# A gated-attention and MLP kernel: the third and fourth unit's matmuls reordered with nine more warm-ups, and two strided access patterns turned round

## The chip, the cores and the metric

The kernel runs on one core of a Trainium2 chip. Its time is the device time of one execution in microseconds (us). Three executions before the change took 475.53, 478.7 and 479.36 us; the median, 478.7 us, is what the changed kernel is compared with.

## The reference

Two stages, in float32. The first is a gated linear recurrence for 4 batches x 8 heads, 768 steps, head size 48. The second is a two-layer network on the 3072 resulting rows.

```
f = 1 / (1 + exp(-f_logit))
for t in range(S):
    state = f[:, :, t, :, None] * state + einsum('bhd,bhe->bhde', k[:, :, t], v[:, :, t])
    y[:, :, t] = einsum('bhd,bhde->bhe', q[:, :, t], state)
x = y.transpose(0, 2, 1, 3).reshape(3072, 384)
h = x @ w_in                      # 384 -> 2048
g = h * clip(h + 3, 0, 6) / 6
out = g @ w_out                   # 2048 -> 384
```

## The kernel before, in words

**Units and groups.** The sequence is cut into 6 chunks of 128 steps. A chunk of one batch is a unit (24 units, numbered from 0), and the four units of a chunk make a group of 512 token columns. Units 0 to 3, the first unit of each batch, have an empty state. For each unit VectorE (DVE in the profile) runs a backward scan over the gates (`back`, L350), takes reciprocals (`rend`), runs a forward scan (`fwd`, L374), and keys and queries are scaled (`kmul` L363, `qmul` L379, on VectorE or on GpSimd, POOL in the profile). TensorE (PE) then computes the scores (`att`, L418), which VectorE masks (`mask`, L425); turns the keys (`tk`, L437), which ScalarE (ACT) copies out (`ktok`); multiplies turned keys with values (`kv`, L456), from which the state is carried on (`carry0`, `carry1`: L469 and L476 on ScalarE for units 0 to 3); and multiplies queries with the state (`qs`, L488) and masked scores with values (`av`, L505). ScalarE copies the result as the high half of a float32r pair (`xh`, L524); for the first units TensorE subtracts that high half in PSUM (`ym`, L528), and ScalarE copies the rest (`xl`, L535). `hole` moves 16 rows of heads by DMA to where the network's first product wants them.

**The network.** For each group and each of 16 blocks of 128 hidden units there are nine matmuls `mm1` (L573), `relu` on ScalarE (L583), `g` on VectorE (L587), a split of the result into a high and a low half (`gh` L596, `gl` L600), and nine matmuls `mm2` (L617) into three PSUM banks `o`. All large products are three float32r products of high and low halves. The weights' halves are made on the core from the raw input (`ld`, `cy`, `z`, `mid`, `lim`, `dif`, `top`, `high`, `low`), during the first 110 us. The first three blocks of the first group are done in halves of 256 columns: half `a` for units 0 and 1, half `b` for units 2 and 3 (`mm1a`, `relua`, `ga`, `mm2a` and the same with `b`). Here `relu` (L644) and `g` (L648) work on tiles `th` of 256 columns, and `mm2` (L653) is a plain float32 product, without a split. The products' 512 columns are held with two batches woven together: `turned` reads the first product's input so, and `halves_of` turns the order of the second product's input as it is read. When a group is complete its three banks are copied out (`outs` on ScalarE L687, `outv` on VectorE L685) and stored (`od`); the last group's third bank goes in two halves (`outh`).

**What sets the order.** Each token of the string ORDER (L51) issues one step, in that order, and every engine runs its own instructions strictly in that order (L813). The number behind a second dot is the PSUM bank: 0 and 1 are the two halves of `pair0`, 2 and 3 of `pair1`, 4 is `single`. `warm.n` (L789) issues n bf16 matmuls of zeros of 128x512 into the bank `idle`, whose result nobody reads. Steps that use one PSUM bank from different engines wait for each other (`settle`, L749).

Of the kernel before, what the change touches and what calls it, by code (L numbers as in the profile page):

```python
# [56 lines left out]
warm.1 ym.1 mask.2 kmul.3 rend.3 lowi.0 lim.1 fwd.3 dif.1 qmul.3 warm.1 kv.2.0 tk.3.4 hole.0~carry1.1 loadv.3 load.4  # L57
loadq.4 xl.1 z.2 carry0.2 carry1.2 ktok.3 qs.2.2 av.2 kv.3.0 lim.2 end.3 gate.4 carry0.3 xh.2 carry1.3 hole.1 mid.2
top.1 dif.2 top.2 mm1a.0.4 ym.2 high.1 xl.2 att.3.0 mask.3 warm.1 qs.3.2 warm.1 av.3 lowi.1 mm1a.1.1 ld.3 wd.0~ktok.3
load.5 ld.4~carry0.3 hole.2~wd.0 wd.1 loadq.5 relua.0 high.2 cy.3 xh.3 ym.3 ga.0 relua.1 xl.3 back.4 gate.5 z.3 cy.4  # L60
mid.3 rend.4 kmul.4 lowi.2 hole.3 ld.5 wd.2~hole.3 ga.1 lim.3 dif.3 back.5 mm2a.0 mm1a.2.1 mm2a.1 end.4 lim.4 end.5
z.4 mm1b.0.2 mm1b.1.0 mm1b.2.3 relub.0 relua.2 relub.1 top.3 fwd.4 qmul.4 cy.5 high.3 kmul.5 gb.0 ga.2 gb.1 tk.4.4
ktok.4 z.5 mm2b.0 tk.5.0 mm2a.2 ld.6~relub.0 mid.4 dif.4 top.4 mid.5 low.3 rend.5 high.4 relub.2 ktok.5 lim.5 low.4
fwd.5 dif.5 mm1.3.2 mm2b.1 att.4.0 mm1.4.4 cy.6 lim.6 mid.6 top.5 dif.6 decay.5 gb.2 mm2b.2 loadv.4~cy.5 ld.7
loadv.5~ld.6 loadq.6~loadv.4 z.6 relu.3 top.6 high.5 cy.7 z.7 relu.4 g.3 low.5 decay.4 qmul.5 mask.4 kv.4.2 kv.5.0 g.4
mm1.5.4 carry0.4 carry0.5 carry1.4 carry1.5 gh.3 high.6 load.6~lim.6 ld.8~ld.7 gate.6 ld.9 cy.8 gh.4 relu.5 qs.4.0 z.8
ld.10 loadq.7~z.8 gl.3 back.6 mid.7 low.6 lim.7 att.5.2 av.4 kmul.6 g.5 mask.5 dif.7 gl.4 mm2.3 mm2.4 end.6 lim.8 z.9
gh.5 mid.8 top.7 rend.6 dif.8 top.8 high.7 low.7 gl.5 fwd.6 tk.6.2 ktok.6 cy.9 high.8 low.8 mid.9 mm1.6.3 mm1.7.2
mm1.8.4 load.7~ld.10 ld.11 loadv.6 qmul.6 xh.4 ym.4 z.10 relu.6 g.6 relu.7 gh.6 xl.4 gate.7 g.7 lim.9 mm2.5 qs.5.0
att.6.2 av.5 kv.6.0 gl.6 dif.9 top.9 back.7 cy.10 lim.10 relu.8 mid.10 high.9 z.11 gh.7 xh.5 cy.11 mm2.6 g.8 mask.6  # L70
kmul.7 dif.10 low.9 top.10 high.10 loadv.7 hole.4 ld.12 end.7 cy.12 gh.8 mm1.9.2 mid.11 lim.11 gl.7 dif.11 decay.6
top.11 gl.8 decay.7 mm2.7 tk.7.3 mm2.8 low.10 carry0.6 xl.5 load.8 lim.12 relu.9 g.9 rend.7 carry1.6 ktok.7 z.12 ld.13
ld.14 cy.13 gh.9 fwd.7 mid.12 dif.12 top.12 gl.9 mm1.10.4 qs.6.2 kv.7.0 carry0.7 av.6 qmul.7 z.13 relu.10 xh.6 xl.6
carry1.7 mm2.9 att.7.2 qs.7.0 mid.13 g.10 high.11 cy.14 gate.8 low.11 gh.10 z.14 lim.14 high.12 hole.6 ld.15 load.9
loadv.8 hole.5 mm1.11.4 lim.13 mask.7 gl.10 av.7 mm2.10 dif.13 top.13 mid.14 low.12 xh.7 high.13 relu.11 g.11 low.13
xl.7 cy.15 gh.11 loadv.9 hole.7 loadq.8 loadq.9 loadq.10 mm1.12.2 mm1.13.3 z.15 gl.11 dif.14 top.14 high.14 mid.15
lim.15 dif.15 top.15 low.14 mm2.11 high.15 relu.12 low.15 mm1.14.0 mm1.15.1 mm1.16.4 back.8 g.12 relu.13 relu.14 g.14
rend.8 kmul.8 g.13 gh.12 gate.9 gl.12 end.8 relu.15 gh.13 mm2.12 tk.8.0 gl.13 back.9 fwd.8 mm2.13 gh.14 relu.16 ktok.8
g.15 qmul.8 kv.8.0 att.8.2 load.10 gh.15 kmul.9 decay.8 gl.14 rend.9 mm2.14 gl.15 mask.8 carry0.8 g.16 carry1.8 lowo.0
lowo.2 mm2.15 mm1.17.4 mm1.18.0 mm1.19.1 gh.16 gate.10 outs.0 outs.2 outv.1 fwd.9 gl.16 mm2.16 od.0 tk.9.3 od.2  # L80
relu.17 od.1 back.10 relu.18 end.9 end.10 qmul.9 g.17 rend.10 fwd.10 gh.17 relu.19 ktok.9 g.19 g.18 lowo.1 mm1.20.4
qs.8.0 att.9.2 av.8 kmul.10 qmul.10 decay.9 decay.10 mask.9 gl.17 kv.9.0 mm2.17 tk.10.2 mm1.21.3 xh.8 gh.18 load.11
loadq.11 load.12 loadv.10 gh.19 gl.18 carry0.9 carry1.9 gl.19 xl.8 mm2.18 ktok.10 gate.11 relu.20 relu.21 back.11 g.21
g.20 qs.9.0 att.10.2 av.9 kv.10.0 mm2.19 mm1.22.4 gate.12 back.12 end.12 end.11 gh.20 rend.11 carry0.10 fwd.11 qmul.11
load.13 loadq.12 kmul.11 mask.10 gl.20 tk.11.2 mm2.20 loadv.11 xh.9 relu.22 rend.12 g.22 gh.21 ktok.11 gh.22 gl.21
gl.22 decay.11 fwd.12 carry1.10 mm1.23.4 relu.23 g.23 kmul.12 gate.13 mm2.21 mm1.24.3 gh.23 relu.24 mm2.22 mm1.25.4
qmul.12 gl.23 relu.25 xl.9 g.24 gh.24 qs.10.0 att.11.2 av.10 kv.11.0 xh.10 mask.11 back.13 carry0.11 xl.10 g.25
rend.13 carry1.11 mm2.23 mm1.26.3 tk.12.2 mm1.27.4 ktok.12 relu.26 gl.24 fwd.13 g.26 qs.11.0 att.12.2 av.11 hole.10
load.14 loadv.12 kv.12.0 loadq.13 loadv.13 qmul.13 mask.12 decay.12 gh.25 xh.11 gate.14 relu.27 xl.11 back.14
carry0.12 rend.14 carry1.12 gl.25 mm2.24 hole.11 hole.9 load.15 gh.26 fwd.14 gl.26 g.27 hole.8 loadv.14 loadq.14  # L90
mm1.28.3 mm1.29.2 relu.28 g.28 mm1.30.1 mm1.31.0 mm1.32.3 mm2.25 mm2.26 gh.27 gl.27 mm2.27 gh.28 gl.28 mm2.28 relu.29
end.13 relu.30 kmul.13 g.29 gh.29 kmul.14 g.30 gh.30 gl.29 decay.13 gl.30 tk.13.4 mm2.29 ktok.13 relu.31 g.31 relu.32
tk.14.4 g.32 qs.12.0 att.13.2 av.12 kv.13.0 qmul.14 end.14 ktok.14 gate.15 xh.12 gh.31 decay.14 carry0.13 xl.12
carry1.13 back.15 mask.13 mm1.33.4 mm2.30 qs.13.0 kv.14.2 av.13 hole.12 rend.15 loadq.15 loadv.15 load.16 loadv.16
loadq.16 gl.31 fwd.15 end.15 decay.15 qmul.15 kmul.15 carry0.14 relu.33 g.33 carry1.14 mm2.31 xh.13 xl.13 mm1.34.2
mm1.35.1 tk.15.3 outs.3 gate.16 gh.32 gl.32 back.16 rend.16 od.3 relu.34 gh.33 relu.35 end.16 outs.5 g.34 ktok.15
mm1.36.4 g.35 outv.4 od.5 kmul.16 att.14.2 kv.15.0 gl.33 od.4 relu.36 g.36 carry0.15 carry1.15 mask.14 fwd.16 qmul.16
mm2.32 mm2.33 tk.16.4 gh.34 gh.35 ktok.16 qs.14.2 att.15.0 av.14 kv.16.2 decay.16 gl.35 carry0.16 carry1.16 mask.15
mm1.37.4 xh.14 gl.34 xl.14 mm2.34 qs.15.0 att.16.2 av.15 relu.37 gh.36 gl.36 load.17 load.18 xh.15 mm2.35 mask.16
xl.15 hole.14 loadq.17 hole.15 loadv.17 loadq.18 loadv.18 mm1.38.0 mm1.39.3 mm1.40.2 mm2.36 mm1.41.1 gate.17 gate.18  # L100
back.17 g.37 rend.17 back.18 fwd.17 relu.38 end.17 relu.39 gh.37 gl.37 rend.18 relu.40 kmul.17 fwd.18 kmul.18 g.39
qmul.18 g.40 qmul.17 load.19 hole.13 load.20 mm2.37 tk.17.3 decay.17 g.38 gh.38 ktok.17 gl.38 mm1.42.0 mm2.38 tk.18.2
relu.41 gh.39 gl.39 gh.40 ktok.18 gl.40 g.41 relu.42 g.42 mm1.43.4 relu.43 g.43 mm1.44.2 mm1.45.1 mm1.46.3 mm1.47.0
mm1.48.4 mm2.39 mm2.40 gh.41 gl.41 mm2.41 gh.42 gl.42 mm2.42 relu.44 gh.43 gl.43 g.44 relu.45 relu.46 gh.44 g.45 g.46
gl.44 mm2.43 mm2.44 relu.47 g.47 qs.16.0 att.17.2 av.16 kv.17.0 gh.45 gl.45 mm2.45 gh.46 relu.48 g.48 mm1.49.4 xh.16
end.18 gh.47 gl.46 mm2.46 relu.49 gl.47 g.49 mm1.50.4 relu.50 mm2.47 carry0.17 xl.16 carry1.17 g.50 gh.48 gh.49 outs.6
outs.8 gl.48 outv.7 mask.17 mm1.51.4 od.6 od.8 qs.17.0 att.18.2 av.17 od.7 kv.18.0 relu.51 gl.49 mm2.48 mm2.49 gate.20
xh.17 gh.50 g.51 decay.18 carry0.18 gl.50 carry1.18 mm2.50 gh.51 loadv.19 loadq.19 xl.17 gate.19 gl.51 back.19 rend.19
end.19 mask.18 fwd.19 kmul.19 back.20 mm1.52.4 relu.52 rend.20 g.52 fwd.20 qmul.19 loadv.20 hole.17 loadq.20 mm1.53.0
mm2.51 relu.53 end.20 qmul.20 g.53 kmul.20 decay.19 mm1.54.1 tk.19.2 ktok.19 relu.54 g.54 load.21 load.22 gh.52 gl.52  # L110
gh.53 gate.21 mm1.55.3 relu.55 gl.53 g.55 tk.20.0 ktok.20 mm1.56.4 qs.18.0 att.19.2 av.18 kv.19.0 xh.18 relu.56
mask.19 carry0.19 carry1.19 xl.18 g.56 back.21 decay.20 mm2.52 mm2.53 qs.19.0 att.20.2 av.19 gh.54 gh.55 rend.21 gl.55
gl.54 mask.20 kv.20.0 mm2.54 mm1.57.3 gate.22 end.21 relu.57 fwd.21 hole.16 loadq.21 qmul.21 loadq.22 decay.21 kmul.21
gh.56 gl.56 g.57 carry0.20 mm1.58.4 mm1.59.2 mm2.55 load.23 relu.58 gate.23 tk.21.3 hole.18 loadv.21 loadv.22 ktok.21
# [821 lines left out]
```

## Time and profile before

| | |
|---|---|
| Executions (us) | 475.53, 478.7, 479.36; median 478.7 |
| Profiled execution's own time | 481.13 us |
| Its span | 479.4 us |
| Mean granted TensorE clock | 0.981 |
| Busy: PE, DVE, ACT, POOL | 460.9, 295.9, 225.4, 53.1 us |
| Share of the chain of waits that ended last | PE 80%, DVE 8%, DMA 4%, ACT 4%, issue 2% |
| DMA traffic | 44.91 MB, mean 94 GB/s; the first 12 us at 293 GB/s |

A profile line names the source line, the engine, the operation, the tile written and the tiles read (buffer numbers are left out). A timeline row gives the start in us, the length of a run of like instructions, their count, and in brackets the idle time before them with what ended it; "issue" there is a wait for nothing that the profile shows. A float32 product is two records. A page row of 40 digits cuts the span in 40 slices of 12 us; PEclk is the granted TensorE clock in tenths of full speed. PEld is TensorE's weight load, which runs beside its matmuls.

### The profile page before, as it was taken

The numbers are of one execution on the slowest core, as the hardware profiler recorded it, in microseconds if no ns is written. First come the engines' busy times: TensorE is split into PE (matmuls) and PEld (weight loads), VectorE is DVE, ScalarE is ACT, GpSimd is POOL, SyncE is SP. The second block draws the span as 40 slices with busy tenths as digits, with TensorE's granted clock in tenths as the row PEclk, the third lists the DMA queues.
The fourth block names the chain that finished last, engine by engine and source line by source line (L and its number), as shares of the span: only waits on it lengthen the run. The fifth ranks groups of instructions, "written<-read, shape, count | busy, mean of one in ns | idle before, by whom it ended". The sixth has DMA issues, their size and how long they took to land.

```text
span 479.4 us, 11485 instructions
## 1 busy us (share of the span) xinstructions
PE 460.9 (96%) x4958; PEld 391.5 (82%) x4958; DVE 295.9 (62%) x462; ACT 225.4 (47%) x372; POOL 53.1 (11%) x57
## 2 busy tenths in 40 slices
PE   8879999899999999999999999999999999899994
...
PEclk9959999999999999999999999999999999999998
...
GB/s 293 277 224 214 287 201 183 101 225 58 105 86 84 30 191 0 158 88 146 69 0 2 1 198 77 107 33 2 63 68 10 25 2 0 67 0 1 0 1 72
DMA packets 18969, 44.91 MB, mean 94 GB/s; under 512 B 2528, under 2 KB 8544, under 8 KB 18912
## 3 DMA queue, kind: packets, MB, share of 16 engines
...
q8 instruction: 41, 0.67, 0.6%
q14 instruction: 16, 0.13, 0.1%
q10 hardware_dynamic: 144, 0.13, 0.1%
...
## 4 chain that ended last, share of the span: by engine, by line
PE 80%; DVE 8%; DMA 4%; ACT 4%; issue 2%; SPq 0%; POOL 0%; DVEq 0%; ACTq 0%
PE o L617 32%; PE pair L573 22%; PE single L573 10%; DMA raw<-w 3%; PE pair L488 2%; PE pair L505 2%; PE o L653 2%; PE pair L418 2%; PE pair L456 2%; PE pair L635 1%; PE pair L668 1%; PE single L668 1%; DMA v<-unit 1%; DVE w L285 1%; DVE tg L587 1%
## 5 line engine op out<-in xcount | busy, mean ns | idle before, releaser
L617 PE MATMUL o<-gg,weight 128*128 128x512 f32 x693 | 161.4, 383 | 2.5 <-DVE gg L600 2.4
L617 PEld LDWEIGHTS o<-gg,weight 128*128 128x128 f32 x693 | 128.8, 189 | 22.2 <-DVE gg L600 4.1
L573 PE MATMUL pair<-xts,weight 128*128 128x512 f32 x576 | 132.7, 381 | 0.8 <-DVE weight L293 0.8
L573 PEld LDWEIGHTS pair<-xts,weight 128*128 128x128 f32 x576 | 107.5, 189 | 16.3 <-DVE weight L293 1.2
L600 DVE TENSOR_TENSOR gg<-tg,gg 128x512 fp32r<-128x512 f32 x77 | 53.8, 703 | 58.2 <-ACT gg L596 57.9
L596 ACT ACTIVATE gg<-tg 128x512 fp32r<-128x512 f32 x77 | 48.1, 627 | 82.6 <-PE o L617 59.8
L587 DVE SCALAR_TENSOR_TENSOR tg<-tg,pair 128x512 f32<-128x512 f32 x64 | 42.8, 682 | 48.7 <-ACT tg L583 48.7
L583 ACT ACTIVATE tg<-pair,half 128x512 f32<-128x512 f32 x64 | 43.1, 683 | 54.3 <-PE pair L573 46.2
L573 PE MATMUL single<-xts,weight 128*128 128x512 f32 x261 | 62.2, 383 | 0.0
L573 PEld LDWEIGHTS single<-xts,weight 128*128 128x128 f32 x261 | 48.4, 189 | 6.7
L374 DVE TENSOR_TENSOR_SCAN gates<-gates,rend 112x516 f32<-112x516 f32 x24 | 33.2, 1382 | 0.2
L350 DVE TENSOR_TENSOR_SCAN suffix<-gates,unit 112x516 f32<-112x516 f32 x24 | 30.4, 1265 | 2.8 <-ACT gates L344 2.8
L583 ACT ACTIVATE tg<-single,half 128x512 f32<-128x512 f32 x29 | 19.7, 679 | 22.9 <-PE single L573 19.2
L363 POOL TENSOR_TENSOR qkf<-qkf,suffix 112x512 f32<-112x512 f32 x13 | 17.9, 1375 | 94.9 <-DVE suffix L350 34.4
L524 ACT ACTIVATE xts<-pair 112x512 fp32r<-112x512 f32 x24 | 14.3, 594 | 26.1 <-PE pair L456 12.2
L379 POOL TENSOR_TENSOR qkf<-qkf,gates 112x512 f32<-112x512 f32 x13 | 16.6, 1282 | 81.7 <-PE o L617 46.1
L587 DVE SCALAR_TENSOR_TENSOR tg<-tg,single 128x512 f32<-128x512 f32 x29 | 19.7, 679 | 9.3 <-ACT tg L583 9.3
L617 PE MATMUL o<-xts,weight 128*128 128x512 f32 x96 | 23.7, 381 | 1.6 <-ACT xts L596 1.5
L425 DVE TENSOR_TENSOR a<-pair,causal 128x512 f32<-128x512 f32 x24 | 16.4, 681 | 13.6 <-PE pair L505 8.1
L617 PEld LDWEIGHTS o<-xts,weight 128*128 128x128 f32 x96 | 17.9, 189 | 4.7 <-ACT xts L596 1.9
L537 DVE TENSOR_TENSOR xts<-pair,xts 112x512 fp32r<-112x512 f32 x19 | 13.0, 684 | 10.6 <-ACT xts L524 10.6
L456 PE MATMUL pair<-v,ktok 64*48 64x48 f32 (+1 forms) x768 | 15.0, 213 | 4.7 <-issue 2.7
...
## 6 DMA issues: line engine op xcount, KB each, us to landing
...
```

The source lines that it names most:

```text
L350: nc.vector.tensor_tensor_scan(flat(sf)[:, ::-1], gt[:, 1:][:, ::-1], flat(unit)[:, ::-1], 0.0, op0=ALU.mult, op1=ALU.add,)
L363: engine("kmul", i).tensor_tensor(parts_of(t, 1), parts_of(t, 1), split(sf[:, :, 1:C + 1]), op=ALU.mult)
L374: nc.vector.tensor_tensor_scan(past, past, flat(rend), 0.0, op0=ALU.mult, op1=ALU.add)
L379: engine("qmul", i).tensor_tensor(parts_of(t, 0), parts_of(t, 0), split(to), op=ALU.mult)
L425: nc.vector.tensor_tensor(d["a"].rearrange("r p e t -> r e p t"), d["at"], causal.unsqueeze(1).unsqueeze(1).broadcast_to([128, 2, NP, HC]) ...
L456: nc.tensor.matmul(d["kv"][r:r + m, odd, c, n], d["ktok"][rs, 2 * n + part, r:r + m], heads_of(vt[rs], part, n, e)[:, :D], start=(odd, e) ...
L573: nc.tensor.matmul(h, win(f, a, k), turned(g["xt"][:, k, :g["n"] // C, b]), start=i == 0, stop=i == 3 * KT - 1,)
L583: nc.scalar.activation(d["t"], d["h"], AF.Relu, bias=half, scale=1.0 / 6.0)
L587: nc.vector.scalar_tensor_tensor(d["t"], d["t"], 1.0, d["h"], op0=ALU.min, op1=ALU.mult)
L596: nc.scalar.activation(d["gg"][:, 0], d["t"], AF.Copy)
L600: engine("gl", f if g["name"] == "0" else NU).tensor_tensor(d["gg"][:, 1], d["t"], d["gg"][:, 0].bitcast(F32), op=ALU.subtract)
L617: nc.tensor.matmul(g["o"][m], wout(f, a, m), halves_of(g[f]["gg"][:, b]), start=f == 0 and i == 0, stop=f == NF - 1 and i == 2, skip_group ...
```

## The change

Four edits, two in the table of steps and two in access patterns.

1. Nine more warm-ups: `warm.1` ahead of `kv.2` becomes `warm.6`, and a `warm.2` each is put ahead of `qs.2` and behind `av.2`.
2. `att.3` (the fourth unit's scores) moves from behind `mm1a.0` and `ym.2` to ahead of `kv.3`.
3. The half tiles `th` are held in the order of the output: `relu` and `g` read the PSUM tile with a step of 128 elements and write the tile in a row, and `mm2` reads it in a row. Before, all of that was the other way round.
4. The copies of a finished bank read PSUM with a step of 4 elements and write in a row. Before, they read in a row and wrote with a step of 64 elements.

```
-warm.1 ym.1 mask.2 kmul.3 rend.3 lowi.0 lim.1 fwd.3 dif.1 qmul.3 warm.1 kv.2.0 tk.3.4 ...
+warm.1 ym.1 mask.2 kmul.3 rend.3 lowi.0 lim.1 fwd.3 dif.1 qmul.3 warm.6 kv.2.0 tk.3.4 ...
-... ktok.3 qs.2.2 av.2 kv.3.0 lim.2 ... mm1a.0.4 ym.2 high.1 xl.2 att.3.0 mask.3 ...
+... ktok.3 warm.2 qs.2.2 av.2 warm.2 att.3.0 kv.3.0 lim.2 ... mm1a.0.4 ym.2 high.1 xl.2 mask.3 ...

+    def ranked(x, woven=0):
+        return x.rearrange("p (b c) -> p c b" if woven else "p (c b) -> p c b", b=2)
...
-            nc.scalar.activation(d["t"], d["h"], AF.Relu, bias=half, scale=1.0 / 6.0)
+            nc.scalar.activation(ranked(d["t"]), ranked(d["h"], 1), AF.Relu, bias=half, scale=1.0 / 6.0)
...
-            nc.vector.scalar_tensor_tensor(d["t"], d["t"], 1.0, d["h"], op0=ALU.min, op1=ALU.mult)
+            t = ranked(d["t"])
+            nc.vector.scalar_tensor_tensor(t, t, 1.0, ranked(d["h"], 1), op0=ALU.min, op1=ALU.mult)
...
-                    wout(f, 1, m).bitcast(F32), halves_of(g[f, p]["t"]),
+                    wout(f, 1, m).bitcast(F32), g[f, p]["t"],
...
-            os = os.rearrange("p (h q c) -> p h c q", q=4, c=HC)
-            src = src.rearrange("p (h c q) -> p h c q", q=4, c=HC)
+            os = os.rearrange("p (h q c) -> p h q c", q=4, c=HC)
+            src = src.rearrange("p (h c q) -> p h q c", q=4, c=HC)
```

The first place is TensorE, from the turning of unit 3's keys (`single<-ident`, L437) over unit 2's `qs` and `av` (L488, L505, `pair_71`) to unit 3's `kv` (L456, 24 matmuls of which the first stands here), the first half product (L635, L639 after), unit 2's `ym` (L528) and unit 3's scores (L418, `qkf_328`). Before:

```order
L437 MATMUL single<-ident,qkf_328 128x112 x4
L488 MATMUL pair_71<-qkf_209,middle_102 64x64 x8
L505 MATMUL pair_71<-a_400,v_330 64x64 x8
L505 MATMUL pair_71<-a_400,v_330 48x64 x8
L456 MATMUL pair_70<-v_440,ktok_450 64x48
...
L635 MATMUL single<-xts,weight 128x256 x9
L528 MATMUL pair_71<-xts,minus 112x256 x2
L418 MATMUL pair_70<-qkf_328 64x64 x16
L792 LDWEIGHTS blank
L792 MATMUL idle<-blank 128x512
```

The same place of the changed kernel, where each pair of rows on `blank` stands for two such pairs:

```order
L437 MATMUL single<-ident,qkf_328 128x112 x4
L797 LDWEIGHTS blank
L797 MATMUL idle<-blank 128x512
...
L488 MATMUL pair_71<-qkf_209,middle_102 64x64 x8
L505 MATMUL pair_71<-a_400,v_330 64x64 x8
L505 MATMUL pair_71<-a_400,v_330 48x64 x8
...
L418 MATMUL pair_70<-qkf_328 64x64 x16
L456 MATMUL pair_70<-v_445,ktok_455 64x48
...
L639 MATMUL single<-xts,weight 128x256 x9
L528 MATMUL pair_71<-xts,minus 112x256 x2
```

The scores of unit 3 stand ahead of its `kv`, and two pairs of warm-ups stand on either side of unit 2's `qs` and `av`. Five more pairs stand ahead of unit 2's `kv`, a few rows above. The other engines' order is unchanged.

The second place is ScalarE where the fifth group ends: the copies of its first and third bank (`os<-o`, L687, L692 after), ahead of the first `relu` (L583) of the last group. Before:

```order
L596 ACTIVATE gg_15_4521<-tg_15_4487 128x512
L687 ACTIVATE os_4533<-o_0_4098 128x2x64x4
L687 ACTIVATE os_4533<-o_2_4100 128x2x64x4
L583 ACTIVATE tg_0_4542<-pair_71,half 128x512
L596 ACTIVATE xts<-tg_0_4542 128x512
```

The same place of the changed kernel:

```order
L596 ACTIVATE gg_15_4530<-tg_15_4496 128x512
L692 ACTIVATE os_4542<-o_0_4107 128x512
L692 ACTIVATE os_4542<-o_2_4109 128x512
L583 ACTIVATE tg_0_4551<-pair_71,half 128x512
L596 ACTIVATE xts<-tg_0_4551 128x512
```

Nothing moves here; the two copies write 512 elements in a row instead of runs of four with a step.

More of the change, by code (lines that the diff above doesn't have):

```diff
@@ L56 @@
 cy.1 end.1 carry0.1 carry1.1 gate.3 end.2 high.0 ktok.2 qs.1.2 av.1 xh.1 cy.2 mid.1 qmul.2 back.3 warm.1 att.2.0
[L57 to L114, printed above, removed]
-gh.57 relu.59 xh.19 g.58 xl.19 back.22 kmul.22 g.59 hole.19 mm1.60.4 mm1.61.3 mm2.56 mm1.62.2 mm1.63.0 mm1.64.1 gh.58
@@ L136 @@
-gh.95 mm2m0.94 gl.95 mm2m1.93 mm2m1.94 mm2m0.95 mm2m1.95 outs.15 mm2p.93 od.15 outv.16 mm2p.94 mm2p.95 od.16 mm2q.93
-outh.15 mm2q.94 odh.15 mm2q.95 outh.16 odh.16
+warm.1 ym.1 mask.2 kmul.3 rend.3 lowi.0 lim.1 fwd.3 dif.1 qmul.3 warm.6 kv.2.0 tk.3.4 hole.0~carry1.1 loadv.3 load.4
+loadq.4 xl.1 z.2 carry0.2 carry1.2 ktok.3 warm.2 qs.2.2 av.2 warm.2 att.3.0 kv.3.0 lim.2 end.3 gate.4 carry0.3 xh.2
+carry1.3 hole.1 mid.2 top.1 dif.2 top.2 mm1a.0.4 ym.2 high.1 xl.2 mask.3 warm.1 qs.3.2 warm.1 av.3 lowi.1 mm1a.1.1
@@ new lines @@
+ld.3 wd.0~ktok.3 load.5 ld.4~carry0.3 hole.2~wd.0 wd.1 loadq.5 relua.0 high.2 cy.3 xh.3 ym.3 ga.0 relua.1 xl.3 back.4
+gate.5 z.3 cy.4 mid.3 rend.4 kmul.4 lowi.2 hole.3 ld.5 wd.2~hole.3 ga.1 lim.3 dif.3 back.5 mm2a.0 mm1a.2.1 mm2a.1
+end.4 lim.4 end.5 z.4 mm1b.0.2 mm1b.1.0 mm1b.2.3 relub.0 relua.2 relub.1 top.3 fwd.4 qmul.4 cy.5 high.3 kmul.5 gb.0
+ga.2 gb.1 tk.4.4 ktok.4 z.5 mm2b.0 tk.5.0 mm2a.2 ld.6~relub.0 mid.4 dif.4 top.4 mid.5 low.3 rend.5 high.4 relub.2
+ktok.5 lim.5 low.4 fwd.5 dif.5 mm1.3.2 mm2b.1 att.4.0 mm1.4.4 cy.6 lim.6 mid.6 top.5 dif.6 decay.5 gb.2 mm2b.2
@@ new lines @@
+loadv.4~cy.5 ld.7 loadv.5~ld.6 loadq.6~loadv.4 z.6 relu.3 top.6 high.5 cy.7 z.7 relu.4 g.3 low.5 decay.4 qmul.5 mask.4
+kv.4.2 kv.5.0 g.4 mm1.5.4 carry0.4 carry0.5 carry1.4 carry1.5 gh.3 high.6 load.6~lim.6 ld.8~ld.7 gate.6 ld.9 cy.8 gh.4
+relu.5 qs.4.0 z.8 ld.10 loadq.7~z.8 gl.3 back.6 mid.7 low.6 lim.7 att.5.2 av.4 kmul.6 g.5 mask.5 dif.7 gl.4 mm2.3
+mm2.4 end.6 lim.8 z.9 gh.5 mid.8 top.7 rend.6 dif.8 top.8 high.7 low.7 gl.5 fwd.6 tk.6.2 ktok.6 cy.9 high.8 low.8
+mid.9 mm1.6.3 mm1.7.2 mm1.8.4 load.7~ld.10 ld.11 loadv.6 qmul.6 xh.4 ym.4 z.10 relu.6 g.6 relu.7 gh.6 xl.4 gate.7 g.7
@@ new lines @@
+lim.9 mm2.5 qs.5.0 att.6.2 av.5 kv.6.0 gl.6 dif.9 top.9 back.7 cy.10 lim.10 relu.8 mid.10 high.9 z.11 gh.7 xh.5 cy.11
+mm2.6 g.8 mask.6 kmul.7 dif.10 low.9 top.10 high.10 loadv.7 hole.4 ld.12 end.7 cy.12 gh.8 mm1.9.2 mid.11 lim.11 gl.7
+dif.11 decay.6 top.11 gl.8 decay.7 mm2.7 tk.7.3 mm2.8 low.10 carry0.6 xl.5 load.8 lim.12 relu.9 g.9 rend.7 carry1.6
+ktok.7 z.12 ld.13 ld.14 cy.13 gh.9 fwd.7 mid.12 dif.12 top.12 gl.9 mm1.10.4 qs.6.2 kv.7.0 carry0.7 av.6 qmul.7 z.13
+relu.10 xh.6 xl.6 carry1.7 mm2.9 att.7.2 qs.7.0 mid.13 g.10 high.11 cy.14 gate.8 low.11 gh.10 z.14 lim.14 high.12
@@ new lines @@
+hole.6 ld.15 load.9 loadv.8 hole.5 mm1.11.4 lim.13 mask.7 gl.10 av.7 mm2.10 dif.13 top.13 mid.14 low.12 xh.7 high.13
+relu.11 g.11 low.13 xl.7 cy.15 gh.11 loadv.9 hole.7 loadq.8 loadq.9 loadq.10 mm1.12.2 mm1.13.3 z.15 gl.11 dif.14
+top.14 high.14 mid.15 lim.15 dif.15 top.15 low.14 mm2.11 high.15 relu.12 low.15 mm1.14.0 mm1.15.1 mm1.16.4 back.8 g.12
+relu.13 relu.14 g.14 rend.8 kmul.8 g.13 gh.12 gate.9 gl.12 end.8 relu.15 gh.13 mm2.12 tk.8.0 gl.13 back.9 fwd.8 mm2.13
+gh.14 relu.16 ktok.8 g.15 qmul.8 kv.8.0 att.8.2 load.10 gh.15 kmul.9 decay.8 gl.14 rend.9 mm2.14 gl.15 mask.8 carry0.8
```

78 lines of the change are left out of this document (58 added, 20 removed).

## The prediction

> **What bounds the kernel now.** I read the page's rows by slices first, then busy times by stage, then the timeline of TensorE (PE) where the stages show something odd.
>
> ```profile
> PE   8879999899999999999999999999999999899994
> PEclk9959999999999999999999999999999999999998
> ```
>
> PE is busy nearly everywhere, and its clock is low in one place, the third slice of 12 us. The stages around it, with these columns: length; busy us (and instructions) of PE, PEld, DVE, ACT, POOL; clock; DMA share; GB/s:
>
> ```profile
> 24.56:38.21 13.65, 11.00 (x182) 9.35 (x183) 6.99 (x13) 6.48 (x13) 1.00 (x1) 0.50 0.66 229
> 38.21:58.00 19.79, 19.79 (x138) 15.75 (x141) 18.04 (x29) 19.15 (x29) 5.34 (x4) 1.00 0.73 241
> 84.00:118.00 34.00, 30.87 (x335) 24.94 (x337) 30.94 (x50) 24.15 (x36) 5.47 (x5) 1.00 0.38 132
> 118.00:404.00 286.00, 285.55 (x3174) 248.03 (x3167) 168.16 (x262) 110.46 (x195) 26.93 (x25) 1.00 0.20 65
> ```
>
> From 118 us on PE is the bound (285.55 of 286 us busy at full clock), and nothing in that stage changes but the length of copies on engines that are half idle. From 38.21 to 58 PE, ScalarE (19.15 of 19.79 us) and VectorE (18.04) are all nearly full, so that stage can only start earlier, not shrink much. The first wait that the change can reach is the stretch from 24.56 to 38.21: half clock, PE idle for 2.65 us, ScalarE and VectorE half empty. What PE does there and just before:
>
> ```profile
> 16.30 0.91 PE L456 MATMUL pair<-v,ktok 64*64 64x48 f32 x48 [0.26 <-DMA v<-unit]
> 20.86 0.39 PE L792 MATMUL idle<-blank 128*128 128x512 bf16 x1
> 22.37 1.11 PE L456 MATMUL pair<-v,ktok 64*64 64x48 f32 x48 [1.12 <-DMA v<-unit]
> 24.54 1.13 PE L505 MATMUL pair<-a,v 64*64 64x64 f32 x32
> 25.45 1.14 PE L456 MATMUL pair<-v,ktok 64*64 64x48 f32 x33
> 29.24 0.67 PE L456 MATMUL pair<-v,ktok 64*64 64x48 f32 x15 [2.65 <-issue]
> 29.84 2.29 PE L635 MATMUL single<-xts,weight 128*128 128x256 f32 x9
> 31.92 0.63 PE L528 MATMUL pair<-xts,minus 112*112 112x256 f32 x2
> 32.48 1.13 PE L418 MATMUL pair<-qkf 48*64 48x64 f32 x32
> 34.09 0.71 PE L488 MATMUL pair<-qkf,middle 48*64 48x64 f32 x16
> 35.27 1.14 PE L505 MATMUL pair<-a,v 64*64 64x64 f32 x32
> 36.33 2.15 PE L635 MATMUL pair<-xts,weight 128*128 128x256 f32 x9
> 38.32 0.40 PE L528 MATMUL pair<-xts,minus 112*112 112x256 f32 x2
> ```
>
> Two things happen. PE waits 1.12 us for unit 2's values, and at 24.56 the clock halves. Then `kv.3` breaks off after 33 of 48 records at 26.59 and goes on at 29.24, a wait that nothing in the trace releases ("issue"). The traffic from 26.5 to 29.2, by queue, has
>
> ```profile
> q8 instruction: 1, 0.02, 2.5%
> ```
>
> one block of instructions, and the stretch from 22 to 26.5 has none. I read the gap as PE out of instructions, its next block queued behind data. That is an inference.
>
> The clock by stretches of 3.4 us (same columns):
>
> ```profile
> 21.14:24.56 3.42, 2.21 (x72) 1.64 (x71) 3.42 (x6) 2.36 (x6) 1.29 (x1) 1.00 0.84 230
> 31.38:34.79 3.41, 3.41 (x56) 2.49 (x55) 1.04 (x3) 2.55 (x5) 1.00 (x1) 0.50 0.68 243
> 34.79:38.21 3.42, 3.42 (x43) 2.84 (x43) 2.51 (x5) 0.97 (x2) 0.00 (x0) 0.50 0.63 194
> ```
>
> It fell after a stretch with PE busy 2.21 of 3.42 us, mostly with 64-wide products. It did not come back after one full of small products (31.38 to 34.79), but did after one that held a whole 128-wide half product. So gaps filled with wide work count, and small products count less. The Trainium skill ("TensorE: Matmul & The Clock Gate", section "HAM oscillation — how this bites in real kernels") says that the clock drops only after an idle gap of over about 3.4 us; the trace speaks against it, since the longest gap ahead of the fall is 1.12 us.
>
> **Part 1, warm-ups and scores.** A warm-up streams the 512 columns of a wide product, which from the chain of waits takes 9.71 / 45 = 0.216 us at full clock:
>
> ```profile
> 172.28 9.71 PE pair L573 x45
> ```
>
> The five ahead of `kv.2`, 1.1 us, lie in the wait of 1.12 us that the DMA ends; they cost nothing, and if the values came early, 1.1 us. The two pairs of two cost 0.43 us each ahead of `qs.2` and `att.3`. They end before PE runs dry, so the gap covers them; without the gap they cost 0.86 us. With them the stretch to 24.56 has about 1.5 us more of wide work, and I expect the clock to hold there.
>
> Where does the gap fall? If it comes at the same instruction number, as running dry does, it comes 18 instructions (nine warm-ups with their weight loads) earlier in the work. Before, `kv.3` had issued 33 matmuls and
>
> ```profile
> 25.34 1.19 PEld L456 LDWEIGHTS pair<-v,ktok 64*64 64x64 f32 x34
> ```
>
> 34 loads, 67 instructions; 67 - 18 = 49. Now `att.3` (32 matmuls, 32 loads) stands there, so three quarters of it are done. PE then idles from about 26.2 to 29.24, all but the rest of `att.3` and all of `kv.3` behind it. In that hole the clock has little to hold it up; I let it fall at about 28.
>
> Behind the gap, at half clock and from start to start, before: rest of `kv.3` 0.60, `mm1a.0` 2.08, `ym.2` 0.56, `att.3` 1.07, warm-up 0.54, `qs.3` 0.64, warm-up 0.54, `av.3` 1.06, `mm1a.1` 1.99: 9.08 us, 29.24 to 38.32. After: a quarter of `att.3` 0.27, `kv.3` whole 1.14 + 0.60 = 1.74, and the rest as before: 9.42 us at half clock, 4.71 at full (`kv` takes 0.91 at full against 1.81).
>
> How long is it low? The bounds are nothing and the 13.65 us seen. Now `mm1a.0` and `kv.3` stand together right behind the gap, with `att.3` gone from between the wide pieces, so a dense stretch comes sooner; I take half, 6.8 us, to 34.8. Then 5.55 us of the 9.42 pass at half clock, the other 3.87 in 1.94: `mm1a.1` ends at 36.73 instead of 38.32, 1.6 us earlier.
>
> Does ScalarE let it through?
>
> ```profile
> 29.96 0.33 ACT L469 ACTIVATE middle<-pair 112x192 f32<-112x192 f32 x1 [3.86 <-PE pair L456]
> 30.87 0.85 ACT L290 ACTIVATE weight<-w 128x768 fp32r<-128x768 f32 x1
> 32.59 0.60 ACT L535 ACTIVATE xts<-pair 112x512 fp32r<-112x512 f32 x1 [0.86 <-PE pair L528]
> 34.17 0.99 ACT L260 ACTIVATE top<-raw,lowest 128x768 uint16<-128x768 int16 x1
> 36.47 0.60 ACT L524 ACTIVATE xts<-pair 112x512 fp32r<-112x512 f32 x1 [1.30 <-PE pair L505]
> 38.52 0.47 ACT L644 ACTIVATE th<-pair,half 128x256 f32<-128x256 f32 x1 [1.45 <-PE pair L635]
> ```
>
> Between the end of `kv.3` and `relua.1` its own work is 1.76 (29.96 to 31.72), 2.57 (32.59 to 35.16) and 0.60: 4.93 us. With `kv.3` done at 31.3 it is free at 36.2, ahead of PE. VectorE waits 5.46 us for `att.3` today and follows:
>
> ```profile
> 33.75 0.69 DVE L425 TENSOR_TENSOR a<-pair,causal 128x512 f32<-128x512 f32 x1 [5.46 <-PE pair L418]
> ```
>
> From 38 on the engines are full, so 1.6 us carry through to the end, loads being issued earlier in step. Nothing on SP's or POOL's queue is passed.
>
> **Part 2, half tiles.** Six `relu` and six `g` now read PSUM with a step. No row has that. The nearest is the copy that writes with a step:
>
> ```profile
> L687 ACT ACTIVATE os<-o 128x512 f32<-128x512 f32 x11 | 11.4, 1090 | 8.2 <-PE o L617 8.2
> L583 ACT ACTIVATE tg<-pair,half 128x512 f32<-128x512 f32 x64 | 43.1, 683 | 54.3 <-PE pair L573 46.2 <-DVE gg L600 5.6 <-issue 1.2
> L687 ACT ACTIVATE os<-pair 128x256 f32<-128x256 f32 x1 | 0.6, 603 | 1.6 <-PE pair L668 1.6
> L644 ACT ACTIVATE th<-pair,half 128x256 f32<-128x256 f32 x5 | 2.3, 472 | 1.7 <-PE pair L635 1.6
> ```
>
> 603 against 472 ns for 256 elements: at worst +0.13 each, five in the full stage, +0.65 us; at best nothing. I take nothing. In exchange `mm2` reads in a row:
>
> ```profile
> 38.72 1.63 PE o L653 x6
> 45.99 0.39 PE single L437 x4
> ```
>
> 271 ns a record for 256 columns, where the float32 turn, whose input lies in a row, takes 98 for 112, or 223 for 256. So up to 36 x 0.048 = 1.7 us of PE, but in a stage where ScalarE is full: worth 0 to 0.8, taken as nothing.
>
> **Part 3, copies.** Written in a row, a copy of 512 should take the 683 ns of `relu` instead of 1090. All but two places lie beside PE's work. At the end of the fifth group
>
> ```profile
> 409.93 1.98 ACT L687 ACTIVATE os<-o 128x512 f32<-128x512 f32 x2 [4.77 <-PE o L617]
> 413.79 0.48 PE L617 MATMUL o<-xts,weight 128*128 128x512 f32 x1 [1.52 <-ACT xts L596]
> ```
>
> two copies stand ahead of the `relu` for which PE then idles 1.52 us: 1.98 becomes about 1.25, -0.73 us. The last half copy gains 0.13. Bounds: if a step costs as much on the read side, nothing; if twice that, +0.8.
>
> **Sum.** -1.6 - 0.73 - 0.13 = -2.5 us, from 481.13 to 478.7 for the profiled execution. That one is 2.4 above the median of the runs, so the forecast is 478.7 - 2.5 = **476.2**.
>
> **Rivals.** (a) The clock never falls, because the warm-ups hold it or the gap shrinks. Then PE needs 4.71 us behind the gap, and ScalarE becomes the bound: `kv.3` ends at 30.3, plus 4.93, `relua.1` at 35.2 against 38.52, -3.3. With copies -4.2, and up to 0.8 from the half tiles: 473.7 to 474.5. For it: 1.5 us more of wide work. Against it: a hole of 3 us remains. This is also where the rule of the clock page leads, since 3 us is less than its gap.
> (b) Slower: the clock falls at 28, at the gap, and stays low for 13.65 us as before, to 41.6. Behind the gap 9.42 instead of 9.08, +0.34; then 2.96 us of the full stage run at half clock, +1.48. With the copies' gain, +1.0: 479.7. It decides if no stretch of 3.4 us before 38 is dense enough.
> (c) Reading PSUM with a step costs as much as the step on the write side. The copies gain nothing, `relu` costs +0.65: -1.6 + 0.65, 477.7. The trace shows neither. The Trainium skill ("Advanced Engine Details and Errata", section "PSUM Cachelines") says that PSUM is served in lines of two float32 and that patterns that aren't contiguous slow matmuls significantly; it names matmuls only, and no run here shows it for copies.
>
> **Chances.** Forecast 0.45, (a) 0.25, (b) 0.15, (c) 0.15. The range, 472 to 481, takes in (a) with the whole PE gain and (b) with (c). A measurement of this kernel tells about 1% (4.8 us) from no change, given runs 3.8 us apart. Faster by more than that (under 473.9) needs (a) at its better end: 0.21. Slower by more needs (b) and (c) and more: 0.05. Within: 0.74.
>
> **What would show it.** Clock 1.00 from 21 to at least 27; the "issue" gap inside L418 rather than L456; less than 13.65 us at half clock; `mm1a.1` ending near 36.7; VectorE's wait ahead of L425 shorter than 5.46 us; copies near 0.69 us and PE's wait at 413 near 0.8; `relu` on `th` at 0.47. Wrong if the gap moves or grows, if the clock falls at 24.56 all the same, or if copies stay at 1.08.

## The result, and the profile after

The changed kernel took 472.22 us (median of 4 executions, 471.98 to 473.95) against 478.32 us before (4 executions, 475.53 to 479.36): a ratio of 0.9891, 95% interval 0.9854 to 0.9928. Run again later, on one chip beside its parts, it took 473.78 us (6 executions) against 478.47 (29): 0.9919, interval 0.989 to 0.9948. So it is faster by 4.7 to 6.1 us, about 1%, where the prediction had 2.5. The two profiled executions differ by more, 481.13 against 471.98 us; below it turns out why.

The rows by slices of the changed kernel's page, PE's busy share and its granted clock:

```profile
PE   9889998999999999999999999999999999999995
PEclk9999999999999999999999999999999999999998
```

The clock is full up to the last slice. Its stages, with the columns of the prediction (length; busy us and instructions of PE, PEld, DVE, ACT, POOL; clock; DMA share; GB/s):

```profile
24.56:38.21 13.65, 11.52 (x221) 9.22 (x214) 11.23 (x19) 11.16 (x21) 2.58 (x2) 1.00 0.78 259
38.21:58.00 19.79, 19.46 (x284) 16.83 (x283) 18.85 (x35) 18.07 (x28) 6.22 (x5) 1.00 0.74 262
118.00:404.00 286.00, 285.82 (x3124) 248.50 (x3123) 162.71 (x253) 107.10 (x195) 24.97 (x23) 1.00 0.20 64
```

The stretch from 24.56 to 38.21 stood at half clock before; now, at full clock, it holds more instructions on every engine (PE 221 instead of 182). From 118 us on PE is full as before. PE's timeline at the place that the first two edits touch:

```profile
25.96 0.58 PE L418 MATMUL pair<-qkf 48*64 48x64 f32 x24
27.24 0.34 PE L418 MATMUL pair<-qkf 48*64 48x64 f32 x8 [0.70 <-issue]
27.36 0.91 PE L456 MATMUL pair<-v,ktok 64*64 64x48 f32 x48
28.20 1.27 PE L639 MATMUL single<-xts,weight 128*128 128x256 f32 x9
...
31.96 1.27 PE L639 MATMUL pair<-xts,weight 128*128 128x256 f32 x9
33.18 0.49 PE L528 MATMUL pair<-xts,minus 112*112 112x256 f32 x2
...
35.81 1.46 PE L658 MATMUL o<-th,weight 128*128 128x256 f32 x6
37.92 3.25 PE L639 MATMUL pair<-xts,weight 128*128 128x256 f32 x27 [0.65 <-DMA xts<-xts]
```

The "issue" gap now lies inside `att.3`, after 24 of its 32 matmuls, and lasts 0.70 us instead of 2.65. `mm1a.1` (the row at 31.96) is done by 33.2, where the prediction had 36.7 and the profile before 38.3; VectorE's wait ahead of unit 3's `mask` went from 5.46 to 1.19 us. `mm1b.0` (the row x27) starts at 37.92; in the profile before it started at 42.57. But it now waits for a DMA, `xts<-xts`, which is `hole`, for 0.65 us.

The groups whose access patterns were turned round:

```profile
L692 ACT ACTIVATE os<-o 128x512 f32<-128x512 f32 x11 | 6.2, 591 | 8.2 <-PE o L617 8.2
L658 PE MATMUL o<-th,weight 128*128 128x256 f32 x36 | 8.8, 380 | 0.0
L648 ACT ACTIVATE th<-pair,half 128x256 f32<-128x256 f32 x5 | 2.3, 472 | 0.9 <-PE pair L639 0.7
```

The copies of 512 columns went from 1090 to 591 ns; `relu` on `th` takes 472 ns as before, though it now reads PSUM with a step of 128 elements; a record of the half tiles' `mm2` went from 435 ns (10.8 us in all, the row L653 of before below) to 380. Before, only `mm2` read these tiles with a step; `relu` and `g` read PSUM and wrote the tile in a row. Where the fifth group ends, ScalarE's and PE's timelines:

```profile
403.16 1.09 ACT L692 ACTIVATE os<-o 128x512 f32<-128x512 f32 x2 [4.77 <-PE o L617]
...
406.26 1.21 PE L617 MATMUL o<-xts,weight 128*128 128x512 f32 x3 [0.76 <-ACT xts L596]
```

The two copies take 1.09 us instead of 1.98, and PE's wait is halved, from 1.52 to 0.76.

### The profile page after: what moved, and what is told of

It is laid out like the page before. It is cut to its first block, busy times and chain, and to the rows that moved or that the text cites. A ratio compares the mean times of both kernels' runs of the same rounds, so it can differ in the third digit from the quotient of the medians.

```text
span 470.3 us, 11504 instructions
## 1 busy us (share of the span) xinstructions
PE 456.4 (97%) x4967; PEld 387.9 (82%) x4967; DVE 292.8 (62%) x462; ACT 220.8 (47%) x372; POOL 53.1 (11%) x57
## 4 chain that ended last, share of the span: by engine, by line
PE 79%; ACT 8%; DVE 7%; DMA 3%; issue 2%; POOL 1%; SPq 0%; DVEq 0%; ACTq 0%
PE o L617 33%; PE pair L573 23%; PE single L573 10%; DMA raw<-w 3%; PE pair L488 2%; PE pair L505 2%; PE pair L418 2%; PE pair L456 2%; ACT weight L290 1%; ACT top L260 1%; PE pair L673 1%; PE single L673 1%; DVE w L285 1%; PE idle L797 1%; DVE tg L587 1%
## 5 line engine op out<-in xcount | busy, mean ns | idle before, releaser
L587 DVE SCALAR_TENSOR_TENSOR tg<-tg,pair 128x512 f32<-128x512 f32 x64 | 42.6, 682 | 47.3 <-ACT tg L583 47.3
L583 ACT ACTIVATE tg<-pair,half 128x512 f32<-128x512 f32 x64 | 43.3, 685 | 54.0 <-PE pair L573 47.2
L583 ACT ACTIVATE tg<-single,half 128x512 f32<-128x512 f32 x29 | 19.8, 683 | 25.2 <-PE single L573 20.2
L587 DVE SCALAR_TENSOR_TENSOR tg<-tg,single 128x512 f32<-128x512 f32 x29 | 19.7, 679 | 8.9 <-ACT tg L583 8.9
L260 ACT ACTIVATE top<-raw,lowest 128x768 uint16<-128x768 int16 x16 | 17.8, 1115 | 1.8 <-DMA raw<-w 1.4
```

Of the source, the lines that this page charges most:

```text
L260: nc.scalar.activation(y, top, AF.Relu, bias=lowest)
L583: nc.scalar.activation(d["t"], d["h"], AF.Relu, bias=half, scale=1.0 / 6.0)
L587: nc.vector.scalar_tensor_tensor(d["t"], d["t"], 1.0, d["h"], op0=ALU.min, op1=ALU.mult)
```

## The experiments

Each kernel is the kernel before with the edits named. Short diffs stand with the first use; combinations are those lines together. The times are medians, with the ratio to executions of the kernel before on the same chip.

**The kernel before, once more.** No edit.

> The kernel before once more, for how far its own executions differ: if the gap and the fall of the clock belong to the program, the same gap at PE's instruction 961 and a fall of the clock within one stretch of 3.4 us of 24.56; if they are chance, another picture. The end of the span 6.6 us behind the last matmul if that belongs to the kernel, nearer 5 if not.

Its profiled execution took 481.14 us, within 0.01 of the first. PE's timeline, though, isn't the same:

```profile
29.69 0.67 PE L456 MATMUL pair<-v,ktok 64*64 64x48 f32 x15 [1.34 <-issue]
30.29 2.29 PE L635 MATMUL single<-xts,weight 128*128 128x256 f32 x9
...
35.52 1.27 PE L635 MATMUL pair<-xts,weight 128*128 128x256 f32 x9
...
42.35 2.92 PE L635 MATMUL pair<-xts,weight 128*128 128x256 f32 x24 [1.06 <-DMA xts<-xts]
```

The gap comes after the same 33 matmuls of `kv.3`, but lasts 1.34 us; the half clock ends between the two half products `mm1a` (2.29 us, then 1.27), after 6.8 us instead of 13.65. And yet `mm1b.0` starts at 42.35, only 0.22 earlier: what the clock gave back went into a wait for `hole`. The two transfers of unit 3's `hole` were issued 1.7 us earlier than in the first profile (37.81 and 38.44 instead of 39.50 and 40.13), but took longer; the DMA engines were 79% busy with data from 37 to 42.5 us here, against 34% from 39 to 43 there. Their rows among the DMA issues (count, size, median us from issue to landing), in the first profile of before and in this one:

```profile
xts<-xts SPq DMA_DIRECT2D x2, 48.0 KB, 2.2
```

```profile
xts<-xts SPq DMA_DIRECT2D x2, 48.0 KB, 4.0
```

The second of them landed at 42.21 instead of 42.34, and `mm1b.0` starts 0.14 us behind that. So the low stretch and the gap vary from execution to execution of one kernel, and their loss is not simply the time that the program loses.

**The warm-ups alone, all nine or the first five.**

```
-... qmul.3 warm.1 kv.2.0 tk.3.4 ... ktok.3 qs.2.2 av.2 kv.3.0 ...
+... qmul.3 warm.6 kv.2.0 tk.3.4 ... ktok.3 warm.2 qs.2.2 av.2 warm.2 kv.3.0 ...
```

> Only the nine warm-ups. Theory 1 (the clock falls because the stretch ahead of 24.56 us holds too little wide work, and the gap is PE running out of instructions at a fixed instruction number): the clock stays at 1.00 past 24.56 us, at least to 28; the gap comes 18 instructions earlier in the work, in kv.3 (L456) after about 24 of 48 records instead of 33; half clock for under 7 us in all; time 3 to 5 us under before (ratio 0.990 to 0.994). Theory 2 (the scores ahead of kv.3 are what shortens the hole, the warm-ups only fill a wait): the clock still halves near 24.6, the gap stays 2.6 us at the same record of kv.3, time within 1 us of before.

> Only the five warm-ups ahead of kv.2. If the idle 1.1 us ahead of kv.2 is what lets the clock fall (theory 1): the clock is at 1.00 at least to 28 us, the gap comes 10 instructions earlier in the work (kv.3 after about 28 records), time 2.5 to 5 us under before. If the four others are needed as well: the clock falls near 24.6 or 28 for over 6 us, time within 1.5 us of before.

Nine: 478.29 us, ratio 0.9992 (0.9963 to 1.0022). Five, with only the first `warm.6`: 478.10, 1.001 (0.9984 to 1.0036). No difference, although the mean granted clock over all executions rose from 0.991 (chip of the nine) and 0.993 (chip of the five) before to 0.995 in both. The 2.5 to 5 us of the first theories are not there, although in the profile of the five the clock stays full to the program's end; in that of the nine it was low for 6.8 us.

**The scores alone, and both edits of the order.**

```
-... av.2 kv.3.0 lim.2 ... ym.2 high.1 xl.2 att.3.0 mask.3 ...
+... av.2 att.3.0 kv.3.0 lim.2 ... ym.2 high.1 xl.2 mask.3 ...
```

> Only att.3 ahead of kv.3. Theory 1: the clock falls at about 24.6 us for about 13.65 us as before; the gap comes at the same instruction number (961 instructions of PE in the records), so right behind att.3, at the first records of kv.3; time within 1 us of before (0.998 to 1.002). Theory 2: the gap shrinks below 1 us, VectorE's wait ahead of the mask (L425) goes from 5.46 to under 2 us, time 2 to 4 us under before.

> The whole reordering (nine warm-ups and the scores), without the two edits of access patterns. Theory 1: clock 1.00 throughout, gap inside the scores (L418) after 24 of 32 records, mm1a.1 done near 33.2 us; against the changed kernel it lacks the half tiles' and copies' gain (about 1.0 + 0.7): 3.5 to 5 us under before.

Scores: 478.05, 0.9983 (0.9954 to 1.0013), and in its profile the clock was low for 13.7 us, as in the first of before. Both: 477.68, 0.9988 (0.9955 to 1.0021). Part 1 of the prediction, -1.6 us, is not in the times.

**The half tiles alone.** `relu`, `g` and `mm2` as in the change.

```
...
-                    wout(f, 1, m).bitcast(F32), halves_of(g[f, p]["t"]),
+                    wout(f, 1, m).bitcast(F32), g[f, p]["t"],
...
```

> Only the half tiles in output order. Theory 1 (a float32 product that reads its moving tile with a step takes 271 ns a record instead of 217 for 256 columns): the 36 records of mm2 on half tiles come 0.216 to 0.22 us apart, relu and g on them stay at 0.47 and 0.41 us; time 0.3 to 1.0 us under before, since ScalarE and VectorE are full there. Theory 2 (the 271 ns are the weight load of a float32 product): spacing stays 0.27, time the same, or up to 0.6 over if reading PSUM with a step is dear.

477.19, 0.9973 (0.9944 to 1.0003): -1.3 us, with no difference just inside the interval. The profiles tell it apart better, below.

**The copies alone.**

```
-            os = os.rearrange("p (h q c) -> p h c q", q=4, c=HC)
-            src = src.rearrange("p (h c q) -> p h c q", q=4, c=HC)
+            os = os.rearrange("p (h q c) -> p h q c", q=4, c=HC)
+            src = src.rearrange("p (h c q) -> p h q c", q=4, c=HC)
```

> Only the copies. Theory 1 (writing with a step is dear, reading PSUM with one is not): copies 0.59 us on ScalarE and 0.69 on VectorE, the wait of PE near 413 us from 1.52 to 0.76, the last half copy 0.39 instead of 0.60; in all 0.75 + 0.2 = about 1.0 us under before. Theory 2 (the end of the program gains more, because the last stores start earlier and the last block of instructions comes in sooner): 1.0 + 1.3 = 2.3 us under before, from the last matmul to the end of the span 5.0 us instead of 6.6.

475.15, 0.9948 (0.9916 to 0.998): -2.5 us by the ratio, -3.1 by the medians: the whole forecast of the change, or more. That is the second theory's 2.3 us rather than the first's 1.0.

**The change without the warm-ups.**

> The changed kernel without its nine warm-ups. Theory 1: the clock falls near 24.6 us, 13.65 us at half; what is left is the half tiles and the copies: 1 to 2 us under before, 4 to 5 over the changed kernel. Theory 2 (warm-ups only fill): as the changed kernel, 6 us under before.

474.31 on 478.21, 0.9916 (0.9893 to 0.994). Against the changed kernel's 0.9891 this left open whether the warm-ups pay once the two access patterns are turned. Hence four kernels on one chip, all with the half tiles and the copies: with neither edit of the order, with the warm-ups, with the scores, and with both (the changed kernel).

> Only the half tiles and the copies, no warm-ups and no moved scores. Adding the two edits measured alone (-1.3 and -2.5 us on 478.2) gives 474.4 us, ratio 0.992. Theory 1 (the edits add up, and the reordering is worth 0.6 us or less): the changed kernel is then at most 0.6 us below this one, 473.8. Theory 2 (the warm-ups pay once the later stages are shorter, because then the time that the clock gives back is no longer lost to a wait): the changed kernel lies about 2 us below this one, 472.2. If the half tiles and the copies cover the same time: 475.5 or more.

> The nine warm-ups, the half tiles and the copies, the scores left where they were. Theory 1: 474.0, ratio 0.991, within 0.6 us of the kernel with half tiles and copies alone. Theory 2: 472.3, ratio 0.988, about 2 us below it. A mean granted clock over the run near 0.998 under both; where theory 1 holds, the clock is raised and the time does not follow.

> The moved scores, the half tiles and the copies, without the nine warm-ups, now on the same chip as the changed kernel. Theory 1: 474.2, ratio 0.992, within 0.6 us of the changed kernel. Theory 2: 474.3, about 2 us above the changed kernel. The mean granted clock near 0.993, below that of the kernels with warm-ups, under both.

> The changed kernel itself, beside its parts. Theory 1: 473.8, ratio 0.991, and all four kernels of this group within 0.7 us. Theory 2: 472.2, ratio 0.988, together with the kernel without moved scores; the two without warm-ups 2 us above.

| half tiles, copies and | us | ratio | interval | mean clock |
|---|---|---|---|---|
| nothing | 474.52 | 0.9923 | 0.9898 to 0.9949 | 0.993 |
| warm-ups | 475.12 | 0.9937 | 0.9915 to 0.996 | 0.998 |
| scores | 475.67 | 0.9939 | 0.9911 to 0.9967 | 0.993 |
| both | 473.78 | 0.9919 | 0.989 to 0.9948 | 0.998 |

Theory 2 falls: the kernel with warm-ups and without the scores should have been 2 us below the first and is 0.6 above it. The scatter, 1.9 us from lowest to highest, is wider than theory 1's 0.7, but has no order in either edit.

A least-squares fit over the 216 executions of all these kernels (a level for each set of runs plus one number for each edit, the five warm-ups counted as 5/9 of the edit, the edits taken to add up) gives, with 95% intervals: warm-ups -0.3 ± 0.5 us, scores -0.1 ± 0.6, half tiles -1.1 ± 0.7, copies -2.7 ± 0.7. They add up to -4.1, of which the access patterns make 3.8.

## Where the time goes, by the profiles

| profiled execution of | clock | `mm1b.0` starts | to `mm1.5` | main stretch | after the last copy |
|---|---|---|---|---|---|
| before | 0.981 | 42.57 | 16.22 | 305.5 | 5.7 |
| before, again | 0.991 | 42.35 | 16.05 | 305.5 | 5.5 |
| warm-ups | 0.988 | 41.36 | 16.05 | 305.5 | 5.8 |
| five warm-ups | 0.996 | 38.93 | 16.22 | 305.5 | 5.1 |
| scores | 0.982 | 43.77 | 16.22 | 305.5 | 5.5 |
| warm-ups, scores | 0.999 | 39.98 | 16.05 | 305.5 | 4.8 |
| half tiles | 0.997 | 38.59 | 15.26 | 305.5 | 5.1 |
| copies | 0.995 | 38.63 | 16.05 | 304.3 | 4.7 |
| half tiles, copies | 0.994 | 38.34 | 15.19 | 304.3 | 4.7 |
| with warm-ups | 0.999 | 39.65 | 15.21 | 304.3 | 4.7 |
| with scores | 0.996 | 39.97 | 15.88 | 304.3 | 4.5 |
| with scores, other chip | 0.991 | 40.62 | 15.14 | 304.3 | 4.5 |
| changed kernel | 0.997 | 37.92 | 15.20 | 304.3 | 4.3 |
| changed kernel, again | 0.998 | 38.92 | 15.20 | 304.3 | 4.6 |

The columns, in us: the start of `mm1b.0`; from there to the first matmul of `mm1.5`; from the 277th matmul on weights (at 108 us in before) to the 1495th, the one behind PE's wait at the end of the fifth group (414 us in before); from the end of ScalarE's last copy to the end of the span.

**Half tiles** are the second column, and one exception aside it falls in two: 16.05 to 16.22 without, 15.14 to 15.26 with. The stretch by engine in before, in the kernel with the copies alone and in that with half tiles and copies:

```profile
42.57:58.79 16.22, 16.22 (x176) 13.01 (x174) 14.69 (x25) 15.88 (x24) 5.14 (x4) 1.00 0.85 287
```

```profile
38.63:54.68 16.05, 16.05 (x174) 12.92 (x173) 14.61 (x25) 14.84 (x22) 4.36 (x4) 1.00 0.82 285
```

```profile
38.34:53.53 15.19, 14.86 (x173) 12.98 (x173) 14.26 (x24) 14.12 (x21) 3.61 (x4) 1.00 0.85 295
```

Without the edit PE is busy in every microsecond of it: 16.22 of 16.22, 16.05 of 16.05. With it PE has 14.86 us to do, and 0.33 us of waiting takes a part of the gain back. The group in before that was shortened:

```profile
L653 PE MATMUL o<-th,weight 128*128 128x256 f32 x36 | 10.8, 435 | 0.0
```

24 of its 36 records lie in this stretch; at 435 - 380 = 55 ns each that is 1.3 us, of which about 1.0 is left at the end of the stretch. The other 12 lie ahead of `mm1b.0`.

**Copies** are the third and the fourth column: 305.5 to 304.3, and 4.8 to 5.8 against 4.3 to 4.7. Of the 1.2 us of the third column 0.76 are PE's wait at the end of the fifth group. The rest lies 60 us earlier, where the fourth group ends. PE's weight loads there, in the kernel with the half tiles alone and then with the copies too:

```profile
345.31 0.22 PEld L488 LDWEIGHTS pair<-qkf,decayed 48*48 48x48 f32 x10 [0.28 <-DVE tg L587]
```

```profile
344.72 0.30 PEld L488 LDWEIGHTS pair<-qkf,decayed 48*48 48x48 f32 x16
```

Half way through `qs` the loads wait for VectorE's `g` (L587), and `g` for a `relu` that stands behind two copies on ScalarE. VectorE's row in the one and in the other:

```profile
343.97 1.28 DVE L587 SCALAR_TENSOR_TENSOR tg<-tg,pair 128x512 f32<-128x512 f32 x2 [1.28 <-ACT tg L583]
```

```profile
343.07 1.28 DVE L587 SCALAR_TENSOR_TENSOR tg<-tg,pair 128x512 f32<-128x512 f32 x2 [0.50 <-ACT tg L583]
```

With the shorter copies `g` is done before `qs` needs it, and the wait on PE is gone. At the program's end the last half copy is shorter by 0.22 us, and the third store that SP issues goes out sooner. In before, and in the changed kernel:

```profile
472.77 2.03 SPq L691 DMA_DIRECT2D outT<-os  x1
```

```profile
465.05 0.33 SPq L696 DMA_DIRECT2D outT<-os  x1
```

The issue takes 0.33 us in all seven profiles with the copies turned, and 1.1 to 2.1 us in six of the seven without; the seventh (warm-ups and scores) has 0.33, and the shortest end of the seven, 4.8. In each of those six it ends 0.2 to 0.4 us after a block of instructions has landed (in before one fetched from 472.55 to 474.38); in the other eight it is over before that block lands. I read it as SP waiting for its next instructions behind the stores' own data, which the earlier issue escapes; no run took that apart. The late store itself lands at most 0.3 us behind the last of ScalarE's; behind the last landing the span goes on for 2.0 to 2.4 us in the six and 1.5 to 1.9 in the others, and what fills that time is open.

**Warm-ups and scores** are the first column, and there is no order in it by these edits: 38.34 with neither, 39.65 with the warm-ups at a clock of 0.999. What the column follows is `hole`: in 11 of the 14 profiles `mm1b.0` starts 0.13 to 0.14 us after the second transfer of unit 3's `hole` has landed, and that transfer takes 2.2 to 4.0 us from issue to landing. The warm-ups do hold the clock: five of the six profiles with five or nine more of them are at full clock up to the program's end, and the sixth lost 6.8 us; of the eight without, seven lost 3.4 to 13.7 us. PE's timeline of the kernel at 39.65:

```profile
27.61 0.56 PE L456 MATMUL pair<-v,ktok 64*64 64x48 f32 x24 [1.37 <-issue]
...
35.21 0.40 PE L528 MATMUL pair<-xts,minus 112*112 112x256 f32 x2 [2.08 <-issue]
...
39.65 0.57 PE L639 MATMUL pair<-xts,weight 128*128 128x256 f32 x3 [0.43 <-ACT top L267]
```

The clock is full, and two "issue" gaps of 3.45 us in all cost more than a low clock does elsewhere. The kernel with neither had no such gap, a lower clock, and this row:

```profile
38.34 3.25 PE L639 MATMUL pair<-xts,weight 128*128 128x256 f32 x27 [0.81 <-DMA xts<-xts]
```

Over 87 executions of the kernel before, the time rises by 0.30 us for each us at half clock (taken as twice the missing share of the mean granted clock, times the execution's time; correlation 0.64). The warm-ups raise the mean clock by 0.004 (alone) to 0.005 (in the group of four), 3.7 to 4.6 us less at half clock, worth 1.1 to 1.4 us by that slope. Against it stand four warm-ups that lie in no wait, 0.86 us by the prediction's price, and five that cost up to 1.1 us when unit 2's values come early. These are estimates, but the sum, -0.5 to +0.9, agrees with the -0.3 that the fit found.

## Why the prediction was right and wrong

It forecast 476.2 us, 2.5 less than before, in a range of 472 to 481. Both medians lie in it (472.22 and 473.78), and on either side of the 1% that the prediction drew: -1.1% and -0.8%. The change gains about twice what was forecast, and mostly not where the prediction put it. That the number came as near as it did is luck: 1.6 us of gain that was forecast is not there, and about 2.9 us that was not forecast is.

- **Part 1, -1.6 us: not there (-0.3 ± 0.7 by the fit, the two edits together).** The step that failed is "From 38 on the engines are full, so 1.6 us carry through to the end". Between `mm1a.1` and the full stage lies the wait of `mm1b.0` for `hole`, and it takes the gain: the second profile of before had `mm1a.1` under way 0.8 us earlier (35.52 instead of 36.33), and `mm1b.0` only 0.22. "Loads being issued earlier in step" did not help: `hole` was issued 1.7 us earlier and landed 0.13 earlier. The first profile of before had hidden this, since there PE came to `mm1b.0` 0.23 us after the landing and did not wait. It was also a poor sample: its clock, 0.981, lies below all 87 later executions of the kernel (0.985 to 0.999, mean 0.992), so the 13.65 us at half clock that Part 1 set out to shorten are seldom lost. No run moved `hole` alone.
- **The gap's place: right.** "Three quarters" of `att.3` were to be done when PE ran dry, and 24 of 32 matmuls were. Eight of the 14 profiles show it at one instruction number (last section). Its length, forecast as about 3 us with the clock falling at 28, was 0.70 and the clock held.
- **Part 2, taken as nothing: -1.1 ± 0.7 by the fit, -0.9 in the stage.** The step that failed is "in a stage where ScalarE is full". The row quoted for it read 19.15 of 19.79 us for ScalarE, and 19.79 of 19.79 for PE. PE was the bound, and ScalarE the next. The size on PE's side was nearly right (up to 1.7 us forecast, 36 x 0.055 = 2.0 measured), and `relu` and `g` paid nothing for reading PSUM with a step.
- **Part 3, -0.86: -2.7 ± 0.7.** The term at the fifth group was right (-0.73 forecast, -0.76 measured). What failed is "All but two places lie beside PE's work": the fourth group's end gives another 0.4, the end of the program about 1 in place of 0.13. Both were read off PE's waits and the copies' own lengths; what stands behind the copies, a `g` that `qs` needs and the issue of a store, was not followed. The three places add up to 2.2 us, within the fit's interval. The copies also got shorter than the 683 ns of `relu`, to 591.
- **Rivals.** (a), the clock never falls, did come true in the profile, and its 473.7 to 474.5 is near the later median; but the clock was not the reason, since the kernel with half tiles and copies alone reaches 474.52 without a warm-up. (b), a low clock for 13.65 us behind the gap, was seen in no profile with warm-ups; the longest there is 6.8 us. (c), PSUM reads with a step as dear as writes, is refuted by 591 ns for the copies and 472 for `relu`. The page "Advanced Engine Details and Errata" of the Trainium skill (section "PSUM Cachelines") warns of non-contiguous PSUM patterns for matmuls; the trace shows no such cost for ScalarE's and VectorE's reads.
- **Why the profiles differ by 9.1 us.** 481.13 lies 2.6 above the mean of 87 executions of before (478.5), and 471.98 is the fastest of the ten of the changed kernel (mean 473.4), 1.4 below it. The rest, 5.1, is the change.

No version beat the changed kernel; the one with half tiles and copies alone can't be told from it.
